# A new load order and finer TensorE pieces in the head of a fused attention and MLP kernel

The chip is one Trainium2 chip, and the program runs on one core of it. The metric is the device time of one execution in microseconds (us); a kernel's time is the median of its runs. PE is TensorE, PEld its weight load, DVE VectorE, ACT ScalarE, POOL GpSimd, SP SyncE. L627 is line 627 of the kernel whose profile is shown; the change shifts the line numbers, so the same score matmuls are L603 before and L627 after.

## The reference

```python
# q, k, v: (batch 8, heads 12, seq 448, dim 64) float32
scores = scale * q @ k.transpose(0, 1, 3, 2) - np.log(S)
attn = 1.0 / (1.0 + np.exp(-scores)) @ v          # sigmoid, no softmax
x = attn.transpose(0, 2, 1, 3).reshape(3584, 768)
h = x @ w_in                                      # 768 -> 2048
g = 0.5 * h * (1 + tanh(c * (h + 0.044715 * h**3)))
out = g @ w_out                                   # 2048 -> 768
```

## The kernel before

The program is written out ahead of time by a small scheduler in Python: it runs a rough model of the engines and the result is one fixed order of instructions for each engine. Four heads of one batch are a *group*, 64 rows of them in each of 7 *strips*; a *unit* is one strip's scores (four 64x448 matmuls into two PSUM banks and one sigmoid over 896 columns). Three groups, 21 units, are batch 0. Batch 0 uses the sigmoid itself; from unit 22 on tanh is used, which shares a table with gelu (the trace has no table load after the one at 25.12 us).

```python
# loads of group 0 (CUTS = strips 0-3 and 4-6 for q and for k alike)
for x, (lo, hi) in enumerate(CUTS):
    both = [ ... e.dma_start(d[:, c:c + w, lo*D:hi*D], ap[:, c:c + w, lo*D:hi*D]) ...
            for (eng, c, w) in ((("SP", 0, 1), ("AQ", 1, 1)) if (nm, x) == ("q", 1) else
                                (("AQ" if nm == "q" else "SP", 0, 2),))]
# loads of group 1: q on ACT's queue, k on SP's
ld[g] = plan.add(Op("ld%s%d" % (nm, g), "AQ" if (nm, g) == ("q", 1) else "SP", ...))
# order of the software queue (v, later q and k with cast, weights w and o)
EARLY = "v0 q2 v1 v2 q3 v3 w0 w1 q4 v4 w2 q5 v5 w3 o0 o1 o2 o3".split()

def make_qk(n, t):                       # one unit of scores
    x, y = take_pair(t)                  # any two free PSUM banks
    for (a, c, half) in ((0, 0, 0), (0, 1, 1), (1, 1, 0), (1, 0, 1)):
        mm(ps[64*half:64*half+64, (x, y)[a], 0:S], kv[...], qv[...])
    # ACT: activation(at, both, AF.Sigmoid)

def make_part(fc, i, t):                 # a third of a first-layer chunk, batch 0 only
    for kt in (2 * i, 2 * i + 1):
        mm(ps[:, bank, 0:S], w_in[:, kt, fc*128:(fc+1)*128], xT[0][:, kt, :], ...)
```

A *chunk* of the first layer is 128 of the 2048 hidden columns, six 448-column matmuls; a *part* is two of them, which need only one group of heads. TensorE runs filler matmuls in the first 11 us to open its clock gate.

## Time and profile before

| | before |
|---|---|
| time, median of 3 | 390.36 us (390.03 to 390.97) |
| PE busy, of the span of 388.1 us | 380.9 us |
| first sigmoid starts / last sigmoid ends | 7.47 / 25.10 us |
| first second-layer matmul | 61.19 us |

The table reads like this: PE is the bound with some 98% of the span, except in the first 26 us, where a row of 21 sigmoids sets the pace. The first second-layer matmul is a good milestone. From 26 us PE has no gap before, so whatever a change wins in the head should show there as a *lead* (how much earlier PE is than in before) and be carried to the end. The profiled run took 389.91 us, 0.45 under the median. Its lines are in the prediction below.

### The profile page before, as it was taken

To read this page: it belongs to the slowest core of one execution; us is meant where nothing else is said; L and a number is where in the kernel's file an instruction comes from. 1 tells how busy PE (TensorE), PEld (TensorE's weight loads), DVE (VectorE), ACT (ScalarE), POOL (GpSimd) and SP (SyncE) were. 2 spreads that over 40 slices of the span, in tenths; PEclk is the share of its full clock that TensorE was granted. 3 is DMA by queue.
4 is the path that set the end of the run, shared out by engine and by line. 5 is a ranking of instruction groups with operands and counts; after the bars stand their busy time and mean duration, and the time that the engine had idled before them with its cause. 6 is when DMAs were issued, how large, how long until landed. Compare 5 with 4: busy or idle time off the path is not lost.

```text
span 388.1 us, 7458 instructions
## 1 busy us (share of the span) xinstructions
PE 380.9 (98%) x3189; PEld 202.4 (52%) x3189; DVE 154.6 (40%) x268; ACT 228.2 (59%) x342; POOL 49.6 (13%) x82
## 2 busy tenths in 40 slices
PE   7899999999999999999999999999999999999996
PEld 5434445545555555555555555555555555555565
DVE  3446633137760276404782068533571541000000
ACT  5999963258764575547684487655674772333221
POOL 5993110001200111001120011101000000000000
PEclk9999999999999999999999999999999999999999
DMA  8999999627791299804899247864472101111133
GB/s 228 195 203 203 210 207 311 138 64 183 188 225 26 59 208 196 200 2 120 184 243 197 47 109 175 219 121 95 113 195 53 42 2 41 43 41 42 41 83 81
DMA packets 64209, 51.74 MB, mean 133 GB/s; under 512 B 36272, under 2 KB 60720, under 8 KB 64176
## 3 DMA queue, kind: packets, MB, share of 16 engines
q1 hardware_dynamic: 48880, 36.77, 37.5%
q0 software_dynamic: 14528, 13.64, 23.1%
q10 hardware_dynamic: 768, 0.86, 0.7%
q8 instruction: 25, 0.41, 0.4%
q14 instruction: 8, 0.07, 0.0%
HBM read 45.61 MB, written 11.01 MB: 146 GB/s over the span
## 4 chain that ended last, share of the span: by engine, by line
PE 94%; ACT 3%; DMA 2%; DVE 0%; ACTq 0%; issue 0%
PE ps L783 38%; PE ps L738 37%; PE ps L603 9%; PE ps L651 8%; ACT at L614 3%; DMA qf<-in_q_dram 2%; PE ps L714 1%; PE ps L560 1%; ACTq L465 0%; DVE qb L355 0%; DVE kb L355 0%; PE ps L557 0%; ACT ob L354 0%
## 5 line engine op out<-in xcount | busy, mean ns | idle before, releaser
L623 ACT ACTIVATE th<-ps 128x896 f32<-128x896 f32 x147 | 127.5, 932 | 52.1 <-PE ps L603 52.1
L783 PE MATMUL ps<-w_out,gT 128*128 128x384 bf16 (+2 forms) x912 | 153.4, 323 | 0.0
L738 PE MATMUL ps<-xT,w_in 128*128 128x448 bf16 x750 | 148.0, 353 | 0.0
L783 PEld LDWEIGHTS ps<-w_out,gT 128*128 128x128 bf16 x912 | 86.9, 98 | 63.4 <-ACT th L623 3.7
L738 PEld LDWEIGHTS ps<-xT,w_in 128*128 128x128 bf16 x750 | 71.4, 98 | 71.9 <-issue 5.6
L627 DVE TENSOR_SCALAR at<-th 128x896 bf16<-128x896 f32 x147 | 91.7, 630 | 40.0 <-ACT th L623 39.0
L752 ACT ACTIVATE gT<-ps 128x448 bf16<-128x448 f32 x128 | 69.5, 554 | 63.7 <-PE ps L738 63.4
L355 DVE COPY ob<-ps 128x384 f32<-128x384 f32 x39 | 21.6, 554 | 75.1 <-PE ps L783 74.8
L603 PE MATMUL ps<-qT,kT 64*64 64x448 bf16 x672 | 48.1, 358 | 2.1 <-ACT at L614 1.7
L489 POOL DMA_DIRECT2D vb<-in_v_dram x24 | 15.0, 623 | 231.4 <-PE ps L603 228.3
L651 PE MATMUL ps<-at,vb 64*64 64x448 bf16 x672 | 38.2, 350 | 0.0
L603 PEld LDWEIGHTS ps<-qT,kT 64*64 64x64 bf16 x672 | 15.5, 105 | 26.5 <-issue 12.8
L354 ACT ACTIVATE ob<-ps 128x384 f32<-128x384 f32 (+2 forms) x18 | 8.5, 472 | 34.2 <-PE ps L783 34.2
L651 PEld LDWEIGHTS ps<-at,vb 64*64 64x64 bf16 x672 | 19.5, 107 | 12.2 <-issue 0.7
L355 DVE CAST kb<-kf 128x896 bf16<-128x896 f32 (+2 forms) x21 | 12.7, 606 | 27.6 <-DMA kf<-in_k_dram 27.6
L355 DVE CAST xT<-ps 128x448 bf16<-128x448 f32 x26 | 15.9, 622 | 11.1 <-PE ps L651 11.1
L614 ACT ACTIVATE at<-ps 128x896 bf16<-128x896 f32 x21 | 17.2, 934 | 1.1 <-PE ps L603 1.1
L355 DVE CAST qb<-qf 128x896 bf16<-128x896 f32 (+1 forms) x20 | 12.4, 618 | 10.7 <-DMA qf<-in_q_dram 10.5
L491 POOL DMA_DIRECT2D vb<-in_v_dram x24 | 15.8, 659 | 0.1
L354 ACT ACTIVATE xT<-ps 128x448 bf16<-128x448 f32 x22 | 12.2, 559 | 1.9 <-PE ps L651 1.9
L840 POOL DMA_DIRECT2D w_in<-in_moe_w_in_dram x16 | 9.9, 656 | 0.0
L412 PE MATMUL ps<-gT,ident 128*128 128x256 bf16 x25 | 5.5, 380 | 1.5 <-POOL ident L362 1.5
(30 smaller groups left out, 43.9 us busy)
## 6 DMA issues: line engine op xcount, KB each, us to landing
out_dram<-ob SPq DMA_DIRECT2D x54, 192.0 KB, 2.8
kf<-in_k_dram SPq DMA_DIRECT2D x19, 448.0 KB, 5.4
qf<-in_q_dram SPq DMA_DIRECT2D x18, 448.0 KB, 6.3
vb<-in_v_dram POOLq DMA_DIRECT2D x48, 112.0 KB, 5.7
w_in<-in_moe_w_in_dram POOLq DMA_DIRECT2D x16, 192.0 KB, 10.7
w_out<-in_moe_w_out_dram POOLq DMA_DIRECT2D x4, 768.0 KB, 21.9
kb<-in_k_dram POOLq DMA_DIRECT2D x4, 224.0 KB, 8.5
qb<-in_q_dram POOLq DMA_DIRECT2D x4, 224.0 KB, 9.0
```

The lines of the kernel that those rows point to most:

```text
L354: return e.activation(o, i, AF.Copy)
L355: return e.tensor_copy(o, i)
L489: a = plan.add(Op("ldv%da" % g, "SWQ", lambda e, d=dst[0:64], ap=lo: e.dma_start(d, ap), deps, 610.0, 0.0, prio=order_v(g), sem="ldv%da" % ...
L491: c = plan.add(Op("ldv%db" % g, "SWQ", lambda e, d=dst[64:128], ap=hi: e.dma_start(d, ap), deps, 610.0, 0.0, prio=order_v(g), sem="ldv%db" ...
L603: r = mm(ps[64 * half:64 * half + 64, (x, y)[a], 0:S], kv[d, a, j, :], qv[d, a, :, :], start=True, stop=True)
L614: lambda e: e.activation(at[as_][:], both, AF.Sigmoid, bias=bias, scale=scale),
L623: lambda e: e.activation(th[ts][:], both, AF.Tanh, bias=0.5 * bias, scale=0.5 * scale),
L627: lambda e: e.tensor_scalar(at[as_][:], th[ts][:], 0.5, 0.5, op0=ALU.mult, op1=ALU.add),
L651: r = mm(ps[64 * c:64 * c + 64, banks[a], 0:S], vb[s][d, slot, j, :], at[as_][d, a, :], start=(j == 0), stop=(j == NJ - 1))
L738: r = mm(ps[:, bank, 0:S], w_in[:, kt, fc * 128:(fc + 1) * 128], xT[xb][:, kt, :], start=(kt == 0), stop=(kt == KT - 1))
L752: lambda e: e.activation(gT[:, fc, col:col + S], ps[:, bank, 0:S], AF.Gelu_apprx_tanh),
L783: r = mm(ps[:, bank, 0:hi - lo], gT[:, fc, col:col + 128], w_out[:, fc, lo:hi], start=(fc == 0), stop=(fc == FC - 1))
```

## The change

Its intent is to start the sigmoids with less data, keep them without a hole, and put more first-layer work under them. The core of the diff:

```diff
-    CUTS = ((0, NJ // 2 + 1), (NJ // 2 + 1, NJ))
+    CUTS = {"q": ((0, NJ // 2 + 1), (NJ // 2 + 1, NJ)), "k": ((0, 3), (3, NJ))}
-    for (eng, c, w) in ((("SP", 0, 1), ("AQ", 1, 1)) if (nm, x) == ("q", 1) else
-                        (("AQ" if nm == "q" else "SP", 0, 2),))
+    for (eng, c, w) in (("AQ" if (nm, x) in (("q", 0), ("k", 1)) else "SP", 0, 2),)
-    ld[g] = plan.add(Op("ld%s%d" % (nm, g), "AQ" if (nm, g) == ("q", 1) else "SP",
+    ld[g] = plan.add(Op("ld%s%d" % (nm, g), "SP",
-    EARLY = ("v0 q2 v1 v2 q3 v3 w0 w1 q4 v4 w2 q5 v5 w3 o0 o1 o2 o3").split()
+    EARLY = ("v0 q2 v1 x0 v2 q3 w0 w1 v3 q4 v4 w2 q5 v5 w3 o0 o1 o2 o3").split()
+    if n == 0:                       # x0: the w_in rows of heads 0 to 3, first 512 columns
+        for c in range(2): ... dma_start(w_in[64*c:64*c+64, 0:2, 0:WSL], ...)
-    HEADS = 3
+    HEADS = (4, 3)                   # chunks begun in parts: 4 of batch 0, 3 of batch 1
+    QK_HOME, AV_HOME, LOW_HOME = (0, 2), (4,), (6, 7)    # PSUM homes during batch 0
-    mm(ps[:, bank, 0:256], ident[:], gT[:, 0, 0:256], ...)      # fillers wait for ident
+    mm(ps[:, bank, 0:w], gT[:, 0, 0:128], gT[:, 0, 0:w], ...)   # fillers wait for a memset only
   ... (banks taken from the homes, parts for batch b, casts of the new pieces: cut)
```

## The prediction

> **What bounds the kernel now.** I read four views of the kernel before: the page (busy shares, chain), busy time by stretch, the timeline of the head, and the waits of TensorE after the head. The stretches come first (columns: length, PE, PEld, DVE, ACT, POOL busy with counts, granted clock, DMA share, GB/s):
> ```profile
> 7.00:11.00 4.00, 3.00 (x35) 1.40 (x34) 2.14 (x5) 3.34 (x4) 4.00 (x7) 1.00 1.18 189
> 11.00:26.00 15.00, 13.43 (x224) 5.98 (x221) 6.01 (x11) 14.76 (x18) 15.00 (x25) 1.00 1.24 200
> 26.00:30.00 4.00, 4.00 (x40) 1.60 (x38) 2.85 (x5) 3.49 (x7) 4.00 (x7) 1.00 1.26 201
> 30.00:40.00 10.00, 10.00 (x130) 4.95 (x129) 6.82 (x13) 9.20 (x15) 2.12 (x3) 1.00 1.25 203
> 40.00:50.00 10.00, 10.00 (x98) 4.32 (x97) 6.48 (x11) 9.93 (x16) 1.39 (x3) 1.00 1.16 211
> ```
> There are two regimes. Until 26 us ACT is full (14.76 of 15.00) and PE is not; from 26 us PE has no gap, and asked for PE's waits from 26 us to the end the profile lists none. So the time is (end of the head) + (PE work not yet done then) + a fixed tail. A change of the head gains only by ending ACT's chain earlier or by doing more of the PE work under it. The timeline says what the head is made of (start, us, engine, line, operation):
> ```profile
> 4.73 0.63 ACT L354 ACTIVATE qb<-qf 128x512 bf16<-128x512 f32 x1 [0.95 <-DMA qf<-in_q_dram]
> ...
> 5.34 0.36 DVE L355 CAST qb<-qf 128x384 bf16<-128x384 f32 x1 [0.55 <-DMA qf<-in_q_dram]
> ...
> 6.21 0.60 ACT L354 ACTIVATE qT<-ps 128x512 bf16<-128x512 bf16 x1 [0.86 <-PE ps L557]
> ...
> 7.04 0.57 PE L603 MATMUL ps<-qT,kT 64*64 64x448 bf16 x8
> ...
> 7.47 3.34 ACT L614 ACTIVATE at<-ps 128x896 bf16<-128x896 f32 x4 [0.66 <-PE ps L603]
> ...
> 9.56 0.67 DVE L355 CAST kb<-kf 128x896 bf16<-128x896 f32 x1
> ...
> 10.29 0.56 PE L557 MATMUL ps<-ident,kb 128*128 128x128 bf16 x7 [0.45 <-DVE kb L355]
> ...
> 11.22 13.88 ACT L614 ACTIVATE at<-ps 128x896 bf16<-128x896 f32 x17 [0.41 <-PE ps L603]
> ...
> 25.12 1.28 ACT L619 ACT_TABLE_LOAD   x1
> ...
> 25.82 1.73 PE L714 MATMUL ps<-xT,w_in 128*128 128x448 bf16 x8
> ...
> 27.49 0.57 PE L603 MATMUL ps<-qT,kT 64*64 64x448 bf16 x8
> ```
> The reader should see: load of group 0, cast, transpose, copy out of PSUM, first scores at 7.04, first sigmoid at 7.47; then 21 sigmoids in a row, of which 17 take 13.88 us (0.816 each), with one hole of 0.41 us before the fifth. That hole comes from PE's fixed order: the transposes of k of group 1 stand ahead of the fifth score unit and wait for its cast, which waited for the loads of q and k of group 1, landing at 8.89 and 9.33 us by the trace's completion events (all landing times below are read there). The chain ends at 25.10.
>
> **What the Trainium skill says.** "TensorE: Matmul & The Clock Gate" (how matmuls follow each other, warm) gives N/2.4 + 2.5 ns from one to the next, 189 ns for 448 columns. The trace agrees: 36 of them from 54.37 to 61.19 us, 6.82/36 = 0.189 with one switch of tiling in it, about 0.187 without. Its Part 1 says that the clock gate opens by a free-running window of about 3.4 us. Here the fillers of 256 columns started 0.21 us apart until about 6.5 us and 0.11 after it, so fillers that start half a microsecond earlier need not open it earlier. "TensorEngine Tiling (Array Packing)" (Key Properties) says that changing the tiling mode drains TensorE. Here six 448-column matmuls after a 64x64 burst take 37.13 to 38.37 us, 1.24 against 6 x 0.187 = 1.12, so a switch costs about 0.12. "DMA: Bandwidth & Descriptors" (Arbitration) says that each DMA engine goes round its queues packet by packet. The first k part (256 KB on SP) landed at 4.34 and the first q part (256 KB on ACT's queue) at 4.71, while both queues moved, which agrees.
>
> **The change part by part.** I compared the two programs' instruction orders, and counted on PE, at each score unit, how much of everything else stands ahead of it.
>
> *New head.* Before, all 448 KB of q and 256 KB of k must land before the first scores. Now k brings 192 KB first on SP, q its strips 0 to 3 (256 KB) first on ACT's queue and strips 4 to 6 (192 KB) second on SP. SP therefore carries 384 KB up to the last q byte, against 352 before. Before, SP's second load landed 0.62 us after its first, for 96 KB: about 155 KB/us under sharing. First k: 4.34 less 64 KB at that pace (0.4) = about 4.0. Last q: 4.0 + 192/155 = about 5.2, as before (5.24). ACT now casts and copies 3 strips, not 4: 0.63 and 0.60 become about 0.47 and 0.46, but it starts at 5.2, not 4.73. Chain: 5.2 + 0.5 cast, + 0.1 to PE, + 3 cold transposes and their latency 0.55, + copy 0.46, + 0.2 to PE = 7.0. First sigmoid at about 7.4: **gain 0.0, give or take 0.3**.
>
> *Group 1's loads.* k of group 1 is now SP's third load, after 384 KB rather than fourth after 544, and is cast before q of group 1, not after it. It should land about 8.3 to 8.8 and be cast by 9.5, ahead of the fifth unit, which PE reaches about 9.9. q of group 1 is needed one unit later. The 0.41 hole closes: **gain 0.4**.
>
> *First-layer parts under the chain.* w_in rows for heads 0 to 3 come as two loads between v of group 1 and v of group 2. The order has 8 first-layer matmuls ahead of the last attention product of batch 0, against 4; 16 against 12 ahead of score unit 22; and from unit 33 on the two orders agree except that the new one is 6 matmuls (one whole chunk) further. The 4 lie in idle PE time. The other 2 and one more tiling switch lie after 26 us, where PE is full. Net: 6 x 0.187 - 2 x 0.187 - 0.12 = **gain 0.63**. The total of PE work is unchanged; it is moved, not removed.
>
> *Batch 1 begun in parts.* PE had no gap at the crossing from batch 0 to 1, so there is nothing to win. It is what makes the move safe: before, chunk 15 of batch 0 (1.12 us) covered the copy of batch 1's last heads out of PSUM, from the end of their product to 0.74 later (54.37 to 55.11). Now four partial matmuls cover it, 4 x 0.187 + 0.12 = 0.87. **Loss 0 to 0.1, taken as 0.05**.
>
> *Fixed PSUM homes, finer fillers.* Scores keep banks 0 to 3, attention products 4 and 5, transposes and parts 6 and 7. ACT went through its last 17 sigmoids without a hole already, so the gain is nothing by itself; the price is that the next group's product waits for the copies out of banks 4 and 5 (1.16 us for two). The order puts two score units in between, so it costs nothing on the chain.
>
> *Later loads.* On the software queue (v, later q and k, weights) 192 KB of w_in as stored took 1.0 us in the FIFO; the two early loads are 128 KB each, so k of group 3 lands 1.3 us later: 16.37 + 1.3 = about 17.6. Its transposes stand behind the 14th score unit, which PE reaches about 17.4 (end of the 12th sigmoid): a margin near zero, with some 0.3 of slack before ACT would starve. The rest of the first w_in columns land about 21.7, needed about 21.9. **Loss 0 to 0.3, taken as 0.1**.
>
> Sum: 0.0 + 0.4 + 0.63 - 0.05 - 0.1 = 0.9 us, 0.23% of 390.36. From 26 us on every microsecond carries to the end, as PE has no gap to absorb it: **389.4 us**.
>
> **The rivals.**
> *A late load takes the place of the hole.* For it: the margins above, and a DMA share over 1 from 7 us until 50. PE is in order, so a late k, q or w_in stops the scores behind it. Against: landings follow a steady FIFO, and each score unit leaves about 0.4 us. It would eat 0.3 to 1.0: 389.7 to 390.4.
> *ACT becomes the bound of batch 1.* ACT is 9.93 of 10.00 busy from 40 to 50 us; the new order puts 13 gelus rather than 12 ahead of the last tanh of batch 1. If ACT paced this stage, tanh would end about 0.43 later relative to the chain, but PE would still be a chunk ahead, so most is kept: about 389.6. Against: the pieces of PE there are exactly matmul pace plus switches.
> *The head starts much earlier.* If the shorter first k and the smaller ACT pieces bring the first sigmoid to 7.0, the time is 389.0 or less; with weight fillers starting before the identity is ready, the clock might open before the q transposes. For it: 640 KB needed, not 704. Against: SP carries more than its half.
> *w_out is needed before it lands.* PE reaches the second layer a microsecond earlier, about 60.2 instead of 61.19; the last w_out part landed at 56.37, so this costs nothing.
>
> **Range and chances.** The head's 0.3 either way, the hole's 0.4, the late loads' 0.3, and the spread of the runs before (390.03 to 390.97, so about 0.4 on a median of three) give 388.2 to 390.4. A 2% change is 7.8 us. Of the head's 25.5 us PE is free for some 12 (22 score units and 20 product steps of 0.2, 84 transposes of about 0.06 and 4 first-layer matmuls of 0.187 make about 14), and the change fills less than a tenth of that. Faster by over 2%: 0.01; within 2%: 0.98; slower: 0.01.
>
> **What would show it.** First sigmoid between 7.1 and 7.7 us; 21 sigmoids without the 0.41 hole, ending at 24.6 to 24.9; eight first-layer matmuls before the chain's end; PE without waits afterwards; the second layer beginning at about 60.3 us. It is wrong if the sigmoids break again where transposes wait for k of group 3 (17 to 18 us) or the parts for w_in (21 to 22), or if PE shows waits for copies out of PSUM near 54 us.

## The result, and the profile after

| | before | after |
|---|---|---|
| time beside each other, same chip, 4 runs each | 390.46 (390.03 to 390.97) | 389.79 (389.0 to 390.41) |
| first sigmoid starts, us | 7.47 | 7.56 |
| last sigmoid ends, us | 25.10 | 25.13 |
| lead at the first second-layer matmul, us | | 0.85 (61.19 to 60.33) |
| lead at the last second-layer matmuls, us | | 0.07 |
| span of the profiled run, us | 388.1 | 388.0 |

The ratio of after to before is 0.9981, 95% interval 0.9959 to 1.0003. A ratio here is the mean time of one kernel's fast runs over that of the other's of the same rounds, so it is not quite the ratio of the medians that I quote. As this interval reaches over 1, the comparison alone does not exclude that nothing changed; the later ones of after_swap and swap_again do for the changed kernel with one late exchange, and steps_only does for the one with an even order of PE. Of the 37 runs of the kernel before beside this result and the experiments, 3 took 392.8 to 394.1 us, all beside the first two batches of experiments. They count as fast (under 1.5% above the fastest), pull those ratios down and widen their intervals, which is why I go by medians and give the ratio beside them.

Gain: 0.67 us by medians, where 0.96 was predicted (390.36 to 389.4). The two profiled runs are closer, 389.91 and 389.85, as the last lead of 0.07 says: they show what the head wins and where it goes, not the 0.67 itself. The total looks right. The steps show that it was right for partly wrong reasons. First the stretches of the changed kernel (columns as in the prediction: length, then PE, PEld, DVE, ACT, POOL busy with counts, clock, DMA share, GB/s):

```profile
7.00:11.00 4.00, 3.88 (x55) 2.45 (x55) 2.56 (x5) 3.51 (x6) 4.00 (x8) 1.00 1.24 220
11.00:26.00 15.00, 14.35 (x221) 5.62 (x220) 5.54 (x10) 14.85 (x18) 15.00 (x24) 1.00 1.24 197
```

PE went from 13.43 to 14.35 of 15.00: it is nearly as full as ACT now. Then ACT alone in the head (start, duration, engine, line, operation, and in brackets the idle time before it and who ended it):

```profile
5.62 0.52 ACT L357 ACTIVATE qb<-qf 128x384 bf16<-128x384 f32 x1 [2.32 <-DMA qf<-in_q_dram]
6.58 0.49 ACT L357 ACTIVATE qT<-ps 128x384 bf16<-128x384 bf16 x1 [0.43 <-PE ps L581]
7.56 17.57 ACT L638 ACTIVATE at<-ps 128x896 bf16<-128x896 f32 x21 [0.49 <-PE ps L627]
25.15 1.28 ACT L643 ACT_TABLE_LOAD   x1
```

All 21 sigmoids are one row, so the reported hole of 0.41 us is gone. And yet the row ends at 25.13, not 24.7. From the first sigmoid's start to the last one's end it took 17.63 us before and 17.57 after. The single start times explain it. In nanoseconds, from one sigmoid's start to the next: before mostly 797 to 815 with one 1345 and two of 876 and 877; after mostly 797 to 830 with 875, 899, 1014 and 981. The big hole became several small delays, each too small for the view to break the row. The timeline of PE during the two largest and at the end of the row (same columns):

```profile
12.70 0.38 PE L627 MATMUL ps<-qT,kT 64*64 64x448 bf16 x4 [0.17 <-ACT at L638]
12.89 0.38 PE L675 MATMUL ps<-at,vb 64*64 64x448 bf16 x4
13.21 0.58 PE L584 MATMUL ps<-ident,kb 128*64 128x128 bf16 x14
13.72 0.38 PE L627 MATMUL ps<-qT,kT 64*64 64x448 bf16 x4
13.93 0.36 PE L675 MATMUL ps<-at,vb 64*64 64x448 bf16 x4
14.22 0.58 PE L584 MATMUL ps<-ident,qb 128*64 128x128 bf16 x14
14.73 0.38 PE L627 MATMUL ps<-qT,kT 64*64 64x448 bf16 x4
...
24.28 0.55 PE L750 MATMUL ps<-xT,w_in 128*128 128x448 bf16 x2
24.76 0.38 PE L627 MATMUL ps<-qT,kT 64*64 64x448 bf16 x4
24.98 0.59 PE L675 MATMUL ps<-at,vb 64*64 64x448 bf16 x8
25.50 1.69 PE L750 MATMUL ps<-xT,w_in 128*128 128x448 bf16 x8
...
27.11 0.38 PE L627 MATMUL ps<-qT,kT 64*64 64x448 bf16 x4
```

Read the start times, not the durations, whose ends are modelled. Between two score units (L627) stand one product (L675) and 14 transposes (L584), with a change of tiling on each side: 12.70 to 13.72 and 13.72 to 14.73, 1.02 and 1.01 us a step. A sigmoid needs 0.80. So ACT waits for PE there. What costs is heavy steps one after the other: a step of 1.02 that stands between lighter ones, 17.75 to 18.77, lengthened its sigmoid step only to 830. At the end of the lines, product plus one part plus two changes of tiling give 0.98. Also seen: the last product runs at 25.17 or so, right after the last sigmoid (it is inside the row of 24.98, which is the two last products), and the first-layer parts start at 25.50. Before, a part stood ahead of the last product and they started at 25.82. That is 0.32 us which the prediction did not have.

The waits of PE after (three of the six lines; what waited for what: us in total, times, longest):

```profile
PE ps L581 <- ACT qb L357: 0.9, 1, 0.9
PE ps L627 <- DVE ob L358: 0.6, 1, 0.6
PE ps L627 <- ACT at L638: 0.4, 2, 0.2
```

The second is the place where the lead of 0.85 us went. It lies at 274 us, far from everything that was changed. The lead is constant up to 269 us and 0.07 after 277. The timeline of DVE in the changed kernel there:

```profile
273.15 0.63 DVE L358 CAST kb<-kf 128x896 bf16<-128x896 f32 x1 [4.72 <-DMA kf<-in_k_dram]
273.70 0.55 DVE L358 COPY ob<-ps 128x384 f32<-128x384 f32 x1
```

and that of PE:

```profile
273.33 0.36 PE L627 MATMUL ps<-qT,kT 64*64 64x448 bf16 x4
274.30 0.38 PE L627 MATMUL ps<-qT,kT 64*64 64x448 bf16 x4 [0.61 <-DVE ob L358]
```

DVE stood idle 4.72 us for the load of k of group 22, while the output in PSUM, ready since about 271.7, waited behind that cast for its copy. PE needed the copy's bank. Before, PE came there 0.85 later and did not wait; the cast and the copy then ran at 273.16 and 273.70, the same to 0.01. "Trainium Architecture — The Big Picture" (Inside one NeuronCore) of the Trainium skill says that each engine has its own instruction stream and that the engines synchronize only through semaphores; this agrees with one stream an engine, and shows that it is kept in order: a copy whose input was ready stood 2.0 us behind a cast whose input was not.

### The profile page after: what moved, and what is told of

Same layout as the page of the kernel before. It is cut to its first block, busy times and chain, and to the rows that moved or that the text cites. A ratio compares the mean times of both kernels' runs of the same rounds, so it can differ in the third digit from the quotient of the medians.

```text
span 388.0 us, 7497 instructions
## 1 busy us (share of the span) xinstructions
PE 381.4 (98%) x3209; PEld 201.8 (52%) x3209; DVE 154.1 (40%) x268; ACT 228.3 (59%) x342; POOL 50.8 (13%) x84
## 4 chain that ended last, share of the span: by engine, by line
PE 93%; ACT 3%; DMA 3%; issue 0%; DVE 0%; SPq 0%
PE ps L819 38%; PE ps L774 36%; PE ps L627 9%; PE ps L675 7%; ACT at L638 3%; DMA kf<-in_k_dram 2%; PE ps L750 2%; DMA qf<-in_q_dram 1%; PE ps L584 1%; DVE ob L358 0%; ACT qb L357 0%; ACT qT L357 0%; SPq L484 0%; PE ps L581 0%; ACT ob L357 0%
## 5 line engine op out<-in xcount | busy, mean ns | idle before, releaser
L774 PE MATMUL ps<-xT,w_in 128*128 128x448 bf16 x738 | 145.8, 353 | 0.0
L774 PEld LDWEIGHTS ps<-xT,w_in 128*128 128x128 bf16 x738 | 70.2, 98 | 70.6 <-issue 6.1
L627 PE MATMUL ps<-qT,kT 64*64 64x448 bf16 x672 | 48.5, 359 | 1.3 <-DVE ob L358 0.6
L675 PE MATMUL ps<-at,vb 64*64 64x448 bf16 x672 | 38.2, 350 | 0.2 <-DVE xT L358 0.2
L627 PEld LDWEIGHTS ps<-qT,kT 64*64 64x64 bf16 x672 | 15.5, 105 | 26.4 <-issue 12.3
L675 PEld LDWEIGHTS ps<-at,vb 64*64 64x64 bf16 x672 | 19.4, 107 | 12.2 <-issue 1.3
L750 PE MATMUL ps<-xT,w_in 128*128 128x448 bf16 x30 | 7.4, 355 | 0.0
```

Of the source, the lines that this page charges most:

```text
L627: r = mm(ps[64 * half:64 * half + 64, (x, y)[a], 0:S], kv[d, a, j, :], qv[d, a, :, :], start=True, stop=True)
L675: r = mm(ps[64 * c:64 * c + 64, banks[a], 0:S], vb[s][d, slot, j, :], at[as_][d, a, :], start=(j == 0), stop=(j == NJ - 1))
L774: r = mm(ps[:, bank, 0:S], w_in[:, kt, fc * 128:(fc + 1) * 128], xT[xb][:, kt, :], start=(kt == 0), stop=(kt == KT - 1))
```

## The experiments

Twelve runs of ten kernels were made in three batches, all correct, all with 5 rounds. Each batch ran on one chip with 11 runs of the kernel before: medians 390.48 (first), 390.41 (second) and 390.17 (third; the only one in which before had no run over 391.0). I had two theories after the result. A: the head's gain of 0.4 was lost to the uneven PE steps. B: a fixed stop near 273 us took back what the head had won. The rival of both was that the parts were worth less than counted.

| run | batch | median (range), us | ratio to before, 95% |
|---|---|---|---|
| after_again | 1 | 389.64 (389.24 to 390.72) | 0.9977 (0.9953 to 1.0001) |
| after_swap | 1 | 389.15 (388.91 to 389.52) | 0.9961 (0.9942 to 0.9981) |
| before_swap | 1 | 389.67 (389.26 to 393.72) | 0.9991 (0.9956 to 1.0026) |
| parts_after_chain | 1 | 390.15 (390.10 to 390.62) | 0.9989 (0.9970 to 1.0009) |
| q_both_queues | 2 | 389.54 (389.24 to 390.36) | 0.9973 (0.9941 to 1.0006) |
| even_steps | 2 | 388.70 (388.65 to 388.82) | 0.9950 (0.9921 to 0.9978) |
| before_k_first | 2 | 390.18 (389.04 to 390.88) | 0.9985 (0.9954 to 1.0016) |
| no_batch1_parts | 2 | 389.71 (389.63 to 390.44) | 0.9978 (0.9949 to 1.0008) |
| steps_only | 3 | 388.90 (388.80 to 389.37) | 0.9970 (0.9957 to 0.9983) |
| even_again | 3 | 388.80 (388.69 to 389.50) | 0.9967 (0.9954 to 0.9980) |
| swap_again | 3 | 389.25 (389.07 to 389.77) | 0.9975 (0.9961 to 0.9989) |
| no_parts | 3 | 391.23 (391.16 to 392.55) | 1.0034 (1.0019 to 1.0048) |

**after_again**: the changed kernel, unaltered.

> The changed kernel once more, unaltered, for a second profile and more times. Theory (a random late wait): the lead of about 0.85 us at the first second-layer matmul (60.3 us against 61.2) comes again, as instruction order fixes it; the wait of 0.6 us for a PSUM copy near 273 us is there in some executions and not in others, so the median lies between 389.3 and 389.9 and the runs scatter by a microsecond. Rival (the lead itself varies with the loads of the head): the first second-layer matmul starts anywhere from 60.0 to 61.2 us and no late wait need show.

389.64 against 390.48, 0.84 us; the interval reaches over 1 here too. The stop was there again (0.4 us, lead from 0.68 to 0.10), so it is no accident of one run. Its head shows something else. k of group 3 landed at 18.40 instead of 17.39, and PE waited for it. The timeline of PE:

```profile
18.45 0.58 PE L584 MATMUL ps<-ident,kb 128*64 128x128 bf16 x14 [0.23 <-DMA kb<-in_k_dram]
```

One step of the sigmoids took 1131 ns where after had 830, and the row took 17.87 us. So the first rival of the prediction, a late load in place of the hole, came true in this one of the eleven profiled runs with the new head, and cost some 0.3 us.

**after_swap**: cast and copy exchanged in DVE's order.

```diff
         plan.run()
+        dve = plan.order["DVE"]
+        for i, op in enumerate(dve[:-1]):
+            if op.name == "castk22" and dve[i + 1].name.startswith("evo"):
+                dve[i], dve[i + 1] = dve[i + 1], op
+                break
```

> The changed kernel with two instructions of VectorE exchanged late in the program: the PSUM copy into the output tile now stands ahead of the cast of k of group 22, which waits for its load. Theory: the wait of TensorE near 273 us is gone, the lead of 0.85 us reaches the end, median 389.2 to 389.6, ratio to before 0.9972 or less, less scatter. Rival (that region is paced by the transfers, which land at 273.1 us in both kernels): the lead is lost there again as another wait, and the median is as that of the unaltered changed kernel.

389.15, 0.49 below after_again, with less than half the scatter (0.61 against 1.48 from lowest to highest). The timeline of DVE now:

```profile
271.71 0.56 DVE L358 COPY ob<-ps 128x384 f32<-128x384 f32 x1 [3.28 <-PE ps L819]
272.81 0.63 DVE L358 CAST kb<-kf 128x896 bf16<-128x896 f32 x1 [0.54 <-DMA kf<-in_k_dram]
```

PE has no wait there, and the lead goes from 0.86 to 0.78 only. The mechanism of the stop is shown: one exchange on DVE removes it.

**before_swap**: the same exchange in the kernel before.

> The same exchange in the kernel before. Theory: in its profile that copy was just in time (ended 274.25, scores went on without a wait), so most of its runs lose nothing there: ratio to before 0.998 to 1.0005. If before too loses time there in many of its runs, it gains about 0.3 us or more, and part of the difference between the two kernels lies in this accident and not in the head.

389.67 against 390.48: before gained 0.81 by medians. The ratio, 0.9991 with an interval over 1, does not decide it, as both kernels have slow outliers. So it is likely, and not shown, that most runs of before lose time at that place too, though its profiled run did not, and that the stop does not separate the two kernels. With it taken out of both, they differ by 0.52 (389.67 to 389.15); with it in both by 0.84 (390.48 to 389.64).

The profiled run of before_swap was by chance the one of 393.72 us, which shows what the slow outliers of the old head are. From its waits of PE, the longest:

```profile
PE ps L557 <- DVE kb L355: 2.0, 1, 2.0
```

and three stretches of 3.41 us (columns as above):

```profile
5.96:9.37 3.41, 1.66 (x19) 0.71 (x17) 0.96 (x3) 2.32 (x3) 3.41 (x6) 1.00 1.13 276
9.37:12.78 3.41, 3.08 (x21) 1.47 (x21) 1.74 (x4) 1.83 (x2) 2.96 (x6) 0.50 1.24 195
12.78:16.20 3.42, 3.42 (x36) 1.88 (x39) 1.25 (x2) 1.83 (x2) 3.42 (x6) 0.50 1.23 194
```

The second part of k landed at 9.06 instead of 7.19, PE stood 2.0 us, and the clock (third number from the end) fell to half for 6.83 us. Its sigmoids ended at 28.55. In the changed kernel that part goes second on ACT's queue; it landed between 5.81 and 6.02 wherever nothing was put ahead of it. Runs of 392.7 us or more: 4 of 49 with the old head (3 of before, and this one), none of 61 with the new head (no_parts came to 392.55, for a reason given there). That is suggestive and not more: only one of the four was profiled, and I set the limit after seeing the runs.

**parts_after_chain**: after_swap, but no first-layer part before the last score unit of batch 0.

```diff
-            if fc or b >= len(heads):
+            if fc or b >= len(heads) or early():
                 return None
```

> The exchanged version of the changed kernel, with no first-layer parts begun until the last scores of batch 0 are issued. Theory (steps of scores, product and parts or transposes take 1.0 us, more than the 0.80 of a sigmoid, and so hold the chain up): the last three steps are light again, the last sigmoid starts about 0.2 us earlier (about 24.0 in place of 24.21), but 6 to 8 matmuls of 0.187 move behind the chain, so the first second-layer matmul starts 0.7 to 1.1 us later than with the parts, and the time is 0.7 to 1.1 us longer. Rival (the parts are worth nothing since the chain pays for them): time equal within 0.2 us.

390.15 against 389.15: the parts under the chain are worth 1.0 us. PE's idle time came back in their place, as its waits say:

```profile
PE ps L627 <- ACT at L638: 1.7, 6, 0.6
```

The last sigmoid started at 24.13 against 24.21 in the changed kernel, not the 24.0 expected, and the first had started 0.10 earlier too: from first start to last end the row took 17.62 against 17.57. So the parts did not visibly lengthen the chain. This is no pure removal, though: the scheduler, planning anew, put the transposes of q of group 3 one score unit earlier, which made a second step of 1014 ns.

**q_both_queues**: after_swap, with the second half of q split over both queues (96 KB each); every other order unchanged.

```diff
-    d[:, c:c + w, lo*D:hi*D], ap[:, c:c + w, lo*D:hi*D]
+    d[:, c:c + r, lo*D:hi*D], ap[:, c:c + r, lo*D:hi*D]      # r = 1 for q's second half
+    if (nm, x) == ("q", 1): ... second row of it on "AQ", ahead of k's second part
```

> The exchanged version of the changed kernel, with the second q load of group 0 (strips 4 to 6, 192 KB) split over the two queues, 96 KB each, as before; every engine's order stays the same. Theory (the new head is no faster because that load stands whole behind k on one queue and lands at 5.5 to 5.6 us, against 5.24 before): it lands at 5.1 to 5.3, the first sigmoid starts at 7.1 to 7.3 in place of 7.43 to 7.56, and the time falls by about 0.2 to 0.3 us to some 388.9. Rival (the landing is set by slow single DMA engines or by the total of bytes, not by the queue): landing and first sigmoid as without the split, same time within 0.1.

q landed at 5.42 instead of 5.60, but k's second part at 7.61 instead of 5.81, and the first sigmoid at 7.46 was hardly early. The clock opened only at 6.02 in this run, so its q transposes ran at half pace. PE then waited for that k (waits of PE):

```profile
PE ps L586 <- DVE kb L358: 1.0, 2, 0.5
```

Time 389.54, 0.39 above after_swap on another chip. The theory that q's place in the queue held the start back found no support: q won 0.18 and k lost 1.80. That is more than the 96 KB put ahead of it explain, so something else delayed k as well, and with the late clock the run does not say what an earlier q is worth.

**even_steps**: after_swap, with PE's order changed by hand (the lines move five products, not the six of the expectation, and one part) so that around units 7 to 12 no product stands in one step with transposes.

```diff
+        for name in ("av0.5", "av0.6"):
+            put(name, "qk1.3")           # put: move it on PE to just before that one
+        for name in ("av1.0", "av1.1"):
+            put(name, "av1.2")
+        put("av1.2", "av1.3")
+        put("a0.0x", "qk2.3")
```

> The exchanged version of the changed kernel, with six product steps and one first-layer part of batch 0 moved to later score units, so that no two steps in a row take TensorE longer than a sigmoid around units 7 to 12; total work and everything after the chain unchanged. Theory (two steps of 1.0 us in a row, each with a product and a transpose, cost the chain 0.1 and 0.22 us at the ninth and tenth sigmoid): those two gaps are back to 0.80, the chain ends 0.3 us earlier (24.8 in place of 25.1), and so does the kernel, about 388.85. Rival (the gaps come from the copies and loads and not from TensorE's order): the gaps stay.

388.70, the best of all, with a range of 0.17 only. The timeline of PE in the stretch shown above:

```profile
12.62 0.38 PE L627 MATMUL ps<-qT,kT 64*64 64x448 bf16 x4 [0.17 <-ACT at L638]
12.94 0.58 PE L584 MATMUL ps<-ident,kb 128*64 128x128 bf16 x14
13.45 0.38 PE L627 MATMUL ps<-qT,kT 64*64 64x448 bf16 x4
13.76 0.58 PE L584 MATMUL ps<-ident,qb 128*64 128x128 bf16 x14
14.27 0.38 PE L627 MATMUL ps<-qT,kT 64*64 64x448 bf16 x4
```

The products stand elsewhere, a step with transposes takes 0.82, and the sigmoids there follow each other at 797 and 798. The row ends at 24.77 (after: 25.13), the first second-layer matmul comes at 59.97 (after: 60.33). Both are 0.36 earlier, of which 0.09 came with an earlier first sigmoid (7.47); the row itself is 0.28 shorter, 17.29 against 17.57. Theory A holds: of the three steps, 899 and 1014 ns are gone. The last step of 0.98 was left in.

**before_k_first**: before_swap, with q of group 1 on SP behind k of group 1, to ask whether that order alone closes the hole.

```diff
-    "AQ" if (nm, g) == ("q", 1) else "SP",
+    "SP",
```

> The exchanged version of the kernel before, with one part of the change alone: k of group 1 is loaded and cast ahead of q of group 1, both on SP's queue. Theory: the hole of 0.55 us before the fifth sigmoid (step 1.35 against 0.80) closes, and since the steps of the kernel before are light, nothing takes it back: the chain ends at about 24.6, the first second-layer matmul starts at about 60.7 (61.2 before), and the time is 0.4 to 0.5 us below the exchanged kernel before, about 389.2. Rival (the chain gives it back later for another reason than the new kernel's heavy steps): chain end near 25.1 as in both kernels.

390.18, where 389.2 was expected: no gain is to be seen. Beside its own runs of before (390.41) it is only 0.23 faster, though it has the exchange that was worth 0.81 in before_swap; whether the order of the loads costs something or the exchange was worth less on this chip is open. The hole shrank from a step of 1345 ns to 1151, and the first sigmoid of this run came at 7.81. PE's order in this plan puts the transposes of q of group 1 ahead of a score unit, and q landed at 9.69. From the waits of PE:

```profile
PE ps L412 <- DVE kT L355: 0.5, 1, 0.5
PE ps L557 <- DVE qb L355: 0.3, 1, 0.3
```

So in this run "k first" did not close the hole by itself; in the changed kernel, with the rest of the new plan, there is none.

**no_batch1_parts**: after_swap with `HEADS = (4, 0)`.

> The exchanged version of the changed kernel without chunks of batch 1 begun in parts: the first chunk of batch 1 waits for all six of its inputs. Theory: its first matmul waits for the copies of the last two heads out of PSUM, so near 54.5 us TensorE waits 0.6 to 0.9 us, all of which reaches the end: about 389.9. Rival (other work covers it): no wait, same time.

389.71, 0.56 above after_swap (another chip). The timeline of PE where batch 1 begins:

```profile
52.94 1.52 PE L675 MATMUL ps<-at,vb 64*64 64x448 bf16 x28
55.28 2.05 PE L774 MATMUL ps<-xT,w_in 128*128 128x448 bf16 x10 [0.82 <-DVE xT L358]
```

Without the parts nothing covers the copy of the last heads out of PSUM. In the changed kernel six matmuls (L750) begin at 54.53 right behind the product, and there is no wait.

**The third batch** asked whether the stop near 273 us is fixed in time (theory B), valued the even order on one chip, and took all parts away.

**steps_only** is the changed kernel with the even order and without the exchange on DVE.

> The changed kernel with the even TensorE order of even_steps, but without the exchange of the cast and the copy on VectorE. If the late stop near 273 us is a fixed time set by the load of k of group 22, the 0.45 us that the even order wins in the head is lost there: about 389.6, as after_again, the last lead near 0.1 us, and a wait for an output copy of about 0.9 to 1.0 us. If the late stop is only scatter, the head's gain stays: about 389.2.

388.90, lower than either number that I had set down. Theory B in its strict form fell. The load of k of group 22 was issued at 266.25 (after: 266.67) and landed at 272.19 (after: 273.13). It waits for buffers that PE frees, so it moves with the lead, and in this run it was also faster. The stop cost 0.28 here (lead 1.28 to 1.00), as the copy still came second. The timeline of DVE:

```profile
272.22 0.63 DVE L358 CAST kb<-kf 128x896 bf16<-128x896 f32 x1 [4.20 <-DMA kf<-in_k_dram]
272.76 0.55 DVE L358 COPY ob<-ps 128x384 f32<-128x384 f32 x1
```

**even_again** and **swap_again** are even_steps and after_swap once more, on one chip.

> The same kernel as even_steps, on the same chip as the next one, so that the even order is valued by one exchange alone: 388.7, and 0.4 to 0.5 below after_swap. If the difference of the earlier two runs came from the two chips, it is under 0.2.

> The same kernel as after_swap, as the partner of even_again: 389.1 to 389.2, no wait near 273 us.

388.80 and 389.25: the even order is worth 0.45, the same as across the chips of the first two batches. With even steps the exchange on DVE adds only 0.10 (388.90 to 388.80). The profiled run of swap_again, at 389.77 its slowest, met the same kind of stop one group later, where the exchange was not made (lead 0.74 to 0.16). The timeline of PE:

```profile
287.93 1.31 PE L774 MATMUL ps<-xT,w_in 128*128 128x448 bf16 x6
289.65 6.98 PE L774 MATMUL ps<-xT,w_in 128*128 128x448 bf16 x36 [0.41 <-DVE ob L358]
```

So there are at least two places, at the k loads of groups 22 and 23, where an output copy on DVE has almost no margin. The old head meets the second too: the profiled run of before_swap lost 0.36 there. What a run loses at these places lay between nothing and 0.8 us.

**no_parts**: after_swap with `HEADS = (0, 0)`.

> after_swap with no first-layer parts at all, neither in batch 0 nor in batch 1. If a matmul of 0.187 us done under the chain is worth its own time, the 8 are worth 1.5 us, plus the batch 1 parts' 0.55: about 391.2. If they only cost step time in the head (the TensorE steps over 0.80 us that even_steps took away), the sigmoid chain ends up to 0.3 earlier without them and the loss is that much smaller: about 390.9. A clean count would be: last sigmoid 23.9 to 24.0 instead of 24.2.

391.23 against 389.25 of swap_again: 1.98 us, near the clean count of 2.05. The rival, that the sigmoids would end earlier without the parts, got nothing: they took 17.63 us from first start to last end, as before, against 17.57 with the parts. Here too the plan was made anew, with the same second step of 1014 ns as in parts_after_chain; both are of transposes and products, not of parts. With before at 390.17 here, this version is 1.06 slower than before. Its slowest run, 392.55, was the profiled one: PE had so much idle time under the chain and before the copies (1.1 us more) that the clock fell to half from 26.59 to 30.00.

## Why the prediction was right, and where it was not

The time (389.4, found 389.79, and 389.64 again), the range and the class held. By its own steps:

1. **New head, 0.0 give or take 0.3: right.** The first sigmoid came at 7.56 against 7.47, within the 7.1 to 7.7. The last q landed at 5.60, not 5.2. Most of that was made up elsewhere: transposes with their latency took 0.38 against 0.55, and the two hand-overs to PE 0.11 against 0.3. In q_both_queues q won 0.18 and k lost 1.80. Fillers begun earlier (1.09 against 1.52 us) need not open the clock earlier, as said: in the profiled runs that record it, it opened at 5.96 to 7.51 with the old head and at 4.04 to 6.58 with the new. The latest, 6.58 in swap_again, had the first sigmoid at 7.68, but 6.11 in no_parts had it at 7.46 and 4.36 in after_swap at 7.56.
2. **Group 1's loads, gain 0.4: the hole closed, the gain did not come.** k of group 1 landed at 7.12, earlier than the 8.3 to 8.8, and the row has no hole. The step that failed is the 0.4 itself: it takes for granted that with the hole closed every other sigmoid follows after 0.80 us, and that the new order of products and transposes, as it says of the fixed homes, "costs nothing on the chain". I had added up PE's work under the chain and found it small in sum. What counts is the steps between two score units: with their two changes of tiling, transposes alone take 0.82 us, product and part 0.98, product and transposes 1.01, and several such steps close together use up the scores by which PE is ahead of ACT. Steps of 0.90, 1.01, 0.88 and 0.98 gave the hole's time back (before had two of 0.88 beside its hole). "The 4 lie in idle PE time" is touched only by the 0.98; without any parts the row was no shorter (17.63). The sum of the view spoke against me already: 13.43 of 15.00 busy left 1.6 us from 11 to 26, not the "some 12" of the prediction's count over 25.5 us, which has no changes of tiling in it. even_steps, which moves only PE's order, makes the row 0.28 shorter and the kernel 0.45 faster.
3. **Parts under the chain, gain 0.63: right kind, too small.** The lead was 0.85 with the sigmoid row ending 0.03 later, so this term came to 0.88. (The lead was 0.68 to 0.86 in the four profiled runs with this order of PE, all against the one profile of before.) Of that 0.88, 0.32 was not foreseen (the last product no longer stands behind a part); the other 0.56 is near the 0.63. parts_after_chain puts the parts under the chain at 1.0 us against running them right after its last scores, and no_parts all parts, those of batch 1 too, at 1.98, both with the plan made anew. The second layer began at 60.33, as said (about 60.3).
4. **Batch 1 in parts, "nothing to win", "makes the move safe": right.** Without them PE waits 0.82 at 55 us and the time rises by 0.56 (across two chips). With them there is no wait, as predicted.
5. **"From 26 us on every microsecond carries to the end": wrong.** It was read from a profile in which PE had no wait, which proves that there was no stop in that run and nothing about the margins. One place lay less than 0.1 us from stopping (the unit began at 274.38 in before and could begin at 274.30), and an earlier PE ran into it. In the profiled run 0.78 of the 0.85 was lost; over the runs the medians still show 0.67 and 0.84. That the late stop hits before as well in most runs is likely from before_swap and not shown; it would be why the comparison survived.
6. **Late loads, 0.1:** k of group 3 landed at 17.39 (17.6 predicted), w_in at 21.12 (21.7), w_out at 56.44. None of them ended a wait of PE in this run; in after_again k of group 3 landed at 18.40 and did, the sign that the prediction had named for 17 to 18 us. The rival in which ACT becomes the bound of batch 1 did not come: PE is 10.00 of 10.00 busy from 40 to 50 us.

So two errors, some 0.4 too much for the sigmoid row (it ends 0.03 later, not 0.4 earlier) and 0.25 too little for the parts, largely cancelled, to a lead of 0.85 where the sum was 0.9; and the late stop probably struck both kernels. That the total came out is luck. (The terms sum to 0.88, which gives 389.5; the 389.4 is a slip of 0.1.) The best version, even_steps, beats both: 1.4 us under before on one chip (388.80 to 390.17) and 1.7 on another.

**Open:** why the load of k of group 22 took 5.6 us in before's profiled run, 6.5 in after's and 5.9 to 6.4 in the others; how often before meets the late stop, as its own slow runs were not profiled; why k of group 3 was late in after_again; whether the rare runs of 393 to 394 us always come from a late part of k; and what exchanging the copies at group 23 too would give. It was not run.

## What to carry to other kernels

Under a chain of equal steps, count the work of the other engine step by step with its mode changes, not in sum: the new order left PE with work to spare in sum and still had several steps close together that were longer than the chain's pace. A view without waits says that no wait happened, not that there was margin: before moving an engine forward, look for in-order engines on which something that it needs stands behind something that waits for a load. Price a part of a change by taking it out of the changed kernel rather than by adding it to the old one: "k first" alone showed no gain, and taking the batch 1 parts out cost half a microsecond where adding them had looked worthless. If the plan is made anew without that part, compare the orders first: other pieces move as well.

## What the Trainium skill lacked or had wrong

- "TensorE: Matmul & The Clock Gate" (Part 1) gives a window of about 3.4 us and says "busy" and "idle" without a share. The runs give no single share either, by PE's busy time (its ends are modelled) in windows of 3.41 us counted from a recorded change of the clock. 1.66 us (before_swap) and 1.81 us (no_parts) were followed by the half clock; 2.16 us (parts_after_chain, from 4.04) were not. 2.90 us (q_both_queues, from 2.61) opened the gate; 3.08 us (before_swap, from 9.37) did not. That the window runs freely agrees: fillers begun at 1.09 us opened it anywhere from 4.04 to 6.58.
- "TensorEngine Tiling (Array Packing)" says that a change of tiling mode drains TensorE and gives no time. Here a unit of four score matmuls takes 0.19 to 0.21 us to a product in the same mode and 0.31 to 0.32 to transposes in another, so about 0.1 a change (0.12 by the count in the prediction), and it decides whether a 0.80 us step holds.
- "ScalarE: Activation LUTs" gives 186 ns + 0.833 ns a column and an overlap of about 93 ns back to back: for 896 columns 932 ns, and 839 from start to start. The trace has 917 for a sigmoid that followed a wait, and 797 from start to start in an unbroken row. Its section "What ACT_TABLE_LOAD costs" gives about 1283 ns for the load, which agrees (1.28), and adds a drain of about 1380 ns, 2.66 us in all (2.7 in its glossary). The drain does not show here: the last sigmoid ended at 25.13, the load began at 25.15 and the next activation at 26.44.
- No page warns that a copy out of PSUM can stand behind a cast that waits for a load on the same in-order engine. Here it held PE for 0.6 us at 274 us.
